# Emptying the transposed units of an attention backward: half by ScalarE and half by VectorE, or one whole unit by each

## The chip, the cores and the metric

The kernel runs on one core of a Trainium2 chip. The metric is the device time of one execution in microseconds (us). The engines are named as in the profile: PE is TensorE (PEld its weight loads), DVE is VectorE, ACT is ScalarE, POOL is GpSimd, SP is SyncE, which only issues transfers here. PSUM is the memory that TensorE writes to; SBUF is the working memory.

## The reference

The forward pass is a parallel transformer block on 2048 rows of 448 features, with 16 heads of 28; the kernel computes its output and the gradients of x and of five weight matrices.

```
xn  = layernorm(x)
q, k, v = split(xn @ wqkv)
p   = softmax(q k^T / sqrt(28));  o = p v
out = x + o @ wo + (silu(xn @ w_gate) * (xn @ w_up)) @ w_down
returns out and vjp(out)(grad_out) for x, wqkv, wo, w_gate, w_up, w_down
```

In the attention backward the scores and exp(scores) are computed again, and for each head ds = exp(scores) * (dO v^T - delta). From them come the sums for dv (exp with dO), dk (ds with q) and dq (ds with k). The last contracts over the keys, and for it ds is needed transposed.

## The kernel before

The program is one long list in which the order on each engine is written by hand; tile pools with a fixed number of buffers give the waits. It has three parts: the forward part with the feed-forward network (up to about 770 us of the profiled execution), the attention backward (about 770 to 1600 us), and a short end that makes dx. The change lies in the attention backward alone.

The backward works through 512 units in a loop over k (line 780). A unit is two heads, 512 keys and 128 query rows. Eight units make a group W; `pos` (0 to 7) is the place in the group; there are 64 groups. Unit k is spread over several turns of the loop:

- In turn k PE makes its scores into a PSUM tile `sd` (line 801, two matmuls on 32 rows each), and ScalarE makes E = exp (line 819).
- In turn k + 1 PE makes the product d of dO and v into another `sd` tile (line 814, two matmuls on the other 64 rows), and VectorE makes ds = d * E (line 831). There are three `sd` buffers.
- In turn k + 3 PE adds the unit to the sums for dv and dk (`acc_mm`, line 694, four matmuls in two pairs).

ds is transposed into `dsT` in two ways. Six units of a group go by a DMA transpose from SyncE's queue (line 833); `ds` has eight buffers, and a buffer is free again when its transpose has landed. The other two, units 1 and 4 (`TQ`), go by TensorE: `pe_transpose` makes eight 128x128 transposes into a PSUM tile `aux`, and `tr_out` copies it to SBUF. The early one (unit 1 of this group) comes at the end of position 6, and the late one (unit 4 of the group before) at position 0 between the scores and the d product.

The tile `aux` has a single buffer, and four uses take turns with it within a group: the late transposes at position 0; at positions 1 to 4 the fillers of a job (`job_mms`: a row block of the output `y`, a `dx` part with 14 matmuls of 448 columns, a part of the wqkv gradient `dwq`, or none), emptied by `job_out` on ScalarE; at position 5 the dq product (`dq_mm`), emptied by VectorE at position 6 (`dq_out`); then the early transposes. There are 16 groups with a `y` job, 32 with `dx`, 12 with `dwq`, and 4 without one.

SyncE's queue also carries the loads of the next chunks (`ck`, `x_c`, line 606 to 612), of the next pair and group (lines 582 and 590), and two more kinds of DMA transpose (lines 707 and 765). GpSimd's queue carries stores.

The functions that the change touches, and what calls them:

Of the kernel before, what the change touches and what calls it, by code (L numbers as in the profile page):

```python
# [37 lines left out]
def kernel(  # L38
# [19 lines left out]
    pe, act, dve, pool, sp = nc.tensor, nc.scalar, nc.vector, nc.gpsimd, nc.sync  # L58
# [70 lines left out]
    for c, (d0, dn) in enumerate(DCH):  # L129
        pool.tensor_copy(  # L130
            out=wq_sb[:dn, c].rearrange("p t g (hh r) -> p t (g hh) r", r=HP)[:, :, :, :DH],
            in_=wst[:dn, c, :].rearrange("p (t h d) -> p t h d", t=3, h=H))
# [4 lines left out]
    for hh in range(4):  # L137
        pool.dma_start(out=wo_pad[HP * hh:HP * hh + DH, :, :D], in_=wo_v[hh])
    dve.tensor_reduce(
        out=r_ones[:], in_=ident_f[:].rearrange("p (a b) -> p a b", b=HP)[:, :, 28:30],  # L140
# [102 lines left out]
    for b in range(4):  # L243
        sp.dma_start_transpose(
            out=dyT[:, 4 * b:4 * b + 4].rearrange("p t c s -> p (t c) s"),
            in_=dy_sp[:, 4 * b:4 * b + 4, :].rearrange("p t d -> p (t d)"))
# [238 lines left out]
    def load_w(nm, parts):  # L485

        t = wp.tile([P, NFC, D], BF16, name="W")
        src = {"wd": B_w_down.rearrange("(fc p) d -> p fc d", p=P), "wg": wT_d[0], "wu": wT_d[1], "wq": wqT_d}[nm]
        n = 3 * G if nm == "wq" else NFC
        wtile[nm] = t  # L490
        step = n // parts
        q = pool if nm == "wd" else sp
        out = [lambda i=i: q.dma_start(out=t[:, i:i + step, :], in_=src[:, i:i + step, :])
               for i in range(0, n, step)]
        return out
# [79 lines left out]
    def load_pair(pr, parts):  # L575

        g, r = pr // 2, 64 * (pr % 2)
        q = qdp.tile([P, S], BF16, name="QD")
        k = qdp.tile([P, S], BF16, name="KV")
        qd[pr] = (q, k)  # L580
        n = S // parts
        return [lambda i=i, dst=dst, r0=r0, src=src: sp.dma_start(
                    out=dst[r0:r0 + 64, i:i + n], in_=src[g, r:r + 64, i:i + n])
                for r0, srcs in ((0, (qT_d, kT_d)), (64, (dOT_d, vT_d)))
                for dst, src in zip((q, k), srcs) for i in range(0, S, n)]

    def load_group(g, parts):
        spt[g] = [spg.tile([P, NT, P], BF16, name=nm) for nm in ("Qsp", "Ksp", "dOsp")]
        n = NT // parts
        return [lambda i=i, t=t, src=src: sp.dma_start(  # L590
                    out=t[:, i:i + n, :].rearrange("p t c -> p (t c)"), in_=src[g, :, i * P:(i + n) * P])
                for t, src in zip(spt[g], (spq_d, spk_d, spo_d)) for i in range(0, NT, n)]
# [7 lines left out]
    def job_load(i):  # L600
        if i >= len(jobs) or jobs[i] is None:
            return
        j = jobs[i]
        if j[0] == "y":
            t = ckp.tile([P, NFC + G, P], BF16, name="ck")
            sp.dma_start(out=t[:], in_=hd_d[j[1], :, :G + NFC, :])
            x = ckp.tile([P, D], BF16, name="x_c")
            sp.dma_start(out=x[:], in_=x_d[:, j[1], :])
            chunk[i] = (t, x)
        elif j[0] == "dx":  # L610
            t = ckp.tile([P, NFC + G, P], BF16, name="ck")
            sp.dma_start(out=t[:, :NFC], in_=hd_d[j[2], :, G + NFC * (1 + j[1]):G + NFC * (2 + j[1]), :])
            chunk[i] = t
# [53 lines left out]
    def job_out(i, ps):  # L667
        j = jobs[i]
        if j[0] == "dwq":
            dwq_out(j[1], j[2], ps)  # L670
            return
        o = outp.tile([P, D], BF16, name="row_o")
        act.copy(out=o[:], in_=ps[:, :D])
        if j[0] == "y":
            pool.dma_start(out=out0_d[:, j[1], :], in_=o[:])
        else:
            pool.dma_start(out=(pA_d, pB_d)[j[1]][:, j[2], :], in_=o[:])
        if j[0] != "dwq" and j[-1] == NT - 1 and j[:2] != ("dx", 1):
            wload.extend(load_w("wg" if j[0] == "y" else "wu", 7))
# [34 lines left out]
    TQ = (1, 4)  # L714

    def pe_transpose(W, qi):

        ds, dsT = DS[W * UW + qi], st[("dsT", W)]
        ps = ps_x.tile([P, 8, P], BF16, name="aux")
        for i in range(8):  # L720
            pe.transpose(ps[:, i, :], ds[:, i // 4, (i % 4) * P:(i % 4 + 1) * P], ident_bf[:])  # L721
        st["tr"] = (ps, dsT[:, :, :, qi * P:(qi + 1) * P])

    def tr_out(eng):

        ps, dst = st["tr"]
        if eng is act:
            act.copy(out=dst[:, 0], in_=ps[:, 0:4, :])  # L728
        else:
            dve.tensor_copy(out=dst[:, 1], in_=ps[:, 4:8, :])  # L730

    def dq_mm(W, half):
        pr, kc, w, _ = units[W * UW]
# [46 lines left out]
    for k in range(N + 2 * UW):  # L780
        W, pos = k // UW, k % UW
        if k < N:
            pr, kc, w, qi = units[k]
            if k % 64 == 3 and pr + 1 < NPR:
                pload.extend(load_pair(pr + 1, 2))
            if k % 128 == 3 and pr + 2 < NPR:
                gload.extend(load_group(pr // 2 + 1, 2))
            if pos == 0:
                job_load(W + 2)
            if pos == 4:  # L790
                if W == len(jobs) - 1:
                    wload.extend(load_w("wq", 2))
                for lst, n in ((pload, 2), (gload, 1), (wload, 2)):
                    for f in lst[:n]:
                        f()
                    del lst[:n]
            q, kv = qd[pr]
            qt = 8 * w + qi
            s_ps = ps_sd.tile([P, 2, 512], FP32, name="sd")
            for j in range(2):  # L800
                pe.matmul(s_ps[:, j, :], lhsT=q[HP * j:HP * j + HP, qt * P:(qt + 1) * P],  # L801
                          rhs=kv[HP * j:HP * j + HP, kc * 512:(kc + 1) * 512],
                          start=True, stop=True, tile_position=(HP * j, 0))
        late_tr = pos == 0 and 1 <= W <= NW
        if late_tr:
            pe_transpose(W - 1, TQ[1])
        if 1 <= k <= N:
            pr, kc, w, qi = units[k - 1]
            q, kv = qd[pr]
            qt = 8 * w + qi  # L810
            d_ps = ps_sd.tile([P, 2, 512], FP32, name="sd")
            for j in range(2):
                r = 64 + HP * j
                pe.matmul(d_ps[:, j, :], lhsT=q[r:r + HP, qt * P:(qt + 1) * P],  # L814
                          rhs=kv[r:r + HP, kc * 512:(kc + 1) * 512],
                          start=True, stop=True, tile_position=(r, 0))
        if k < N:
            E[k] = ework.tile([P, 2, 512], BF16, name="E")
            act.activation(out=E[k][:], in_=s_ps[:], func=ACT.Exp, scale=SCALE)  # L819
        if late_tr:  # L820
            tr_out(act)
            tr_out(dve)
        job = jobs[W] if W < len(jobs) else None
        if pos == 6 and 2 <= W <= NW + 1:
            dq_out(W - 2)
        if 1 <= k <= N:
            if qi == 0:
                st[("dsT", (k - 1) // UW)] = twin.tile([P, 2, 4, UW * P], BF16, name="dsT")
            dsT = st[("dsT", (k - 1) // UW)]
            DS[k - 1] = dsw.tile([P, 2, 512], BF16, name="ds")  # L830
            dve.tensor_tensor(out=DS[k - 1][:], in0=d_ps[:], in1=E[k - 1][:], op=ALU.mult)  # L831
            if qi not in TQ:
                sp.dma_start_transpose(out=dsT[:, :, :, qi * P:(qi + 1) * P].rearrange("p j c q -> p (j c) q"),
                                       in_=DS[k - 1][:].rearrange("p j c -> p (j c)"))
        while sp_later:
            sp_later.pop(0)()

        if pos == 1:
            if 3 <= k < N + 3:
                acc_mm(k - 3)  # L840
            if job:
                st["aux"] = ps_x.tile([P, 512], FP32, name="aux")
                fillers = job_mms(W, st["aux"])
        if 1 <= pos < 5 and job:
            n = -(-len(fillers) // (5 - pos))
            for f in fillers[:n]:
                f()
            fillers = fillers[n:]
        if pos == 5 and 2 <= W <= NW + 1:
            dq_mm(W - 2, 0)  # L850
            dq_mm(W - 2, 1)
        if pos != 1 and 3 <= k < N + 3:
            acc_mm(k - 3)
        if pos == 4 and job:
            job_out(W, st["aux"])
        if pos == 6 and W < NW:
            pe_transpose(W, TQ[0])
            tr_out(act)
            tr_out(dve)
    while sp_later:  # L860
        sp_later.pop(0)()
# [3 lines left out]
    with ExitStack() as fin:  # L865
# [17 lines left out]
        for c in range(4):  # L883
            ps = ps_sd.tile([P, 2, 512], FP32, name="sd")
# [68 lines left out]
```

## Time and profile before

| what | value |
|---|---|
| time, median of 3 runs | 1677.39 us (1677.09 to 1687.07) |
| profiled execution: its time, its span | 1683.64 us, 1681.9 us |
| mean granted TensorE clock | 0.952 |
| busy share of the span: PE, PEld, DVE, ACT, POOL | 90%, 36%, 67%, 71%, 24% |
| ScalarE halves of the copies (L728) | 128 of 595 ns, 76.2 us |
| VectorE halves of the copies (L730) | 128 of 424 ns, 54.3 us |
| DMA transposes of ds on SyncE's queue (L833) | 384, median 4.1 us from issue to landing |

Lines of the profile name a group of instructions by the line of the kernel, the engine, the operation and the tiles (out<-in), then the count, the busy time, the mean length in ns, and the time that the engine was idle just before them with what ended it. A line of the timeline has the start and the length in us; x2 after it means that two instructions in a row were put together.

### The profile page before, as it was taken

How to read it: one execution, taken by the hardware profiler on the slowest of the kernel's cores; microseconds unless marked ns; L12 is line 12 of the kernel's file. 1: busy time of each engine (PE TensorE's matmuls, PEld its weight loads, DVE VectorE, ACT ScalarE, POOL GpSimd, SP SyncE). 2: the span in 40 equal slices, each digit the busy share in tenths (PEclk: the TensorE clock that was granted, in tenths of full speed). 3: DMA queues.
4: the chain of work that ended last, by engine and by line, in shares of the span. 5: the costliest groups of instructions: out<-in, count | busy, mean ns of one | idle time of the engine just before them, and what ended most of it. 6: DMA issues, size and time to landing. Idle time of an engine off the chain costs nothing. (4 is left out here: it accounts for less than half of the span.)

```text
span 1681.9 us, 32121 instructions
## 1 busy us (share of the span) xinstructions
PE 1519.8 (90%) x12176; PEld 600.7 (36%) x12176; DVE 1131.8 (67%) x1530; ACT 1186.3 (71%) x1346; POOL 400.9 (24%) x664
## 2 busy tenths in 40 slices
PE   3699999999999999696998999999989999999875
PEld 1132333333233333232443335443335433544352
DVE  6365555555555456345887788888878888888736
ACT  2497888888777678574776777777777777777611
POOL 4133334344234333421001101010102101111132
PEclk9699999999998899797999989999999999999998
DMA  4785658687866577548999999999999999999963
GB/s 126 145 181 115 133 121 169 140 169 118 157 131 130 124 136 148 138 93 231 214 208 212 196 175 196 207 196 208 206 202 194 202 202 179 175 195 195 175 239 100
DMA packets 682155, 285.13 MB, mean 170 GB/s; under 512 B 637792, under 2 KB 651088, under 8 KB 682000
## 3 DMA queue, kind: packets, MB, share of 16 engines
q1 hardware_dynamic: 653616, 215.74, 68.7%
q0 software_dynamic: 25808, 64.30, 15.4%
q10 hardware_dynamic: 2576, 3.04, 0.6%
q8 instruction: 95, 1.56, 0.4%
q14 instruction: 60, 0.49, 0.1%
HBM read 67.34 MB, written 63.44 MB: 78 GB/s over the span
## 5 line engine op out<-in xcount | busy, mean ns | idle before, releaser
L831 DVE TENSOR_TENSOR ds<-sd,E 128x1024 bf16<-128x1024 f32 x512 | 607.6, 1217 | 81.5 <-PE sd L814 34.2
L819 ACT ACTIVATE E<-sd 128x1024 bf16<-128x1024 f32 x512 | 520.1, 1031 | 193.4 <-PE sd L814 99.0
L535 ACT ACTIVATE eT<-s_ps 128x1024 bf16<-128x1024 f32 x512 | 518.2, 1025 | 159.8 <-PE s_ps L531 154.5
L801 PE MATMUL sd<-KV,QD 32*128 32x512 bf16 x1024 | 202.1, 391 | 19.2 <-DVE ds L831 8.1
L814 PE MATMUL sd<-KV,QD 32*128 32x512 bf16 x1024 | 202.9, 388 | 10.9 <-DVE ds L831 6.8
L694 PE MATMUL acc<-ds,Qsp 128*32 128x512 bf16 x1024 | 204.5, 395 | 1.2 <-DVE ds L831 1.2
L531 PE MATMUL s_ps<-qT,kT 32*128 32x512 bf16 x1024 | 204.7, 397 | 0.0
L694 PE MATMUL acc<-E,dOsp 128*32 128x512 bf16 x1024 | 204.3, 395 | 0.0
L339 PE MATMUL f_ps<-xnT,wgu 128*128 128x512 bf16 x448 | 135.9, 400 | 24.7 <-DVE w_sb L365 13.0
L378 POOL DMA_DIRECT2D hd_d<-fT x168 | 126.9, 769 | 40.9 <-DVE fT L363 24.9
L531 PEld LDWEIGHTS <-kT 32*128 32x128 bf16 x1024 | 48.2, 91 | 203.7 <-issue 201.7
L664 PE MATMUL aux<-W,ck 128*128 128x448 bf16 x448 | 106.6, 354 | 6.9 <-DVE dsT L730 6.9
L313 PE MATMUL f_ps<-xn_sp,f_sp 128*128 128x448 bf16 x448 | 110.6, 355 | 0.0
L709 POOL DMA_DIRECT2D dqkv_d<-dkv_o x64 | 39.2, 617 | 284.9 <-ACT dkv_o L700 284.8
L801 PEld LDWEIGHTS <-QD 32*128 32x128 bf16 x1024 | 50.2, 91 | 149.0 <-issue 140.5
L511 PE MATMUL o_ps<-eT,v_sp 128*32 128x512 bf16 x1024 | 101.7, 399 | 0.0
L730 DVE COPY dsT<-aux 128x512 bf16<-128x512 bf16 x128 | 54.3, 424 | 61.7 <-ACT dsT L728 61.7
L694 PEld LDWEIGHTS <-dOsp 128*32 128x32 bf16 x1024 | 50.3, 94 | 120.3 <-issue 117.3
L814 PEld LDWEIGHTS <-QD 32*128 32x128 bf16 x1024 | 69.4, 91 | 53.4 <-issue 34.2
L721 PE MATMUL aux<-ident_bf,ds 128*128 128x128 bf16 x1024 | 78.5, 219 | 11.0 <-DVE dq_acc L758 3.5
L743 PE MATMUL aux<-dsT,Ksp 128*32 128x512 bf16 x1024 | 78.3, 405 | 4.1 <-DMA dsT<-ds 2.5
L351 DVE SCALAR_TENSOR_TENSOR g<-t_sb,f_ps 128x512 f32<-128x512 f32 x56 | 38.4, 686 | 64.6 <-ACT t_sb L349 64.5
(130 smaller groups left out, 1803.1 us busy)
## 6 DMA issues: line engine op xcount, KB each, us to landing
hd_d<-fT POOLq DMA_DIRECT2D x168, 128.0 KB, 4.0
ck<-hd_d SPq DMA_DIRECT2D x32, 448.0 KB, 4.2
ck<-hd_d SPq DMA_DIRECT2D x16, 576.0 KB, 5.0
dsT<-ds SPq DMA_TRANSPOSE x384, 4.1
dq_c<-dqkv_d SPq DMA_DIRECT2D x8, 768.0 KB, 4.7
dqkv_d<-dkv_o POOLq DMA_DIRECT2D x64, 64.0 KB, 3.5
W<-wT_d SPq DMA_DIRECT2D x14, 224.0 KB, 3.9
out_dram<-dw_o POOLq DMA_DIRECT2D x28, 96.0 KB, 4.1
```

Source lines behind the costliest of these rows:

```text
L313: pe.matmul(acc[:, :D], lhsT=src[:, 12 * (t // 4) + 4 * wi + t % 4, :], rhs=rhs[:, t, :D], start=(t == 0), stop=(t == NT - 1))
L339: pe.matmul(st[name][:], lhsT=w(c), rhs=src[:, tsl, c, :], start=(c == 0), stop=(c == 3))
L378: pool.dma_start(out=hd_d[tsl, :, G + NFC * wi + fc, :].rearrange("k p s -> p k s"), in_=o[:, wi, :].rearrange("p (k s) -> p k s", k=4))
L511: pe.matmul(o_ps[HP * hh:HP * (hh + 1), :], lhsT=v[:, kt, HP * hh:HP * (hh + 1)], rhs=e[hh // 2][:, hh % 2, :], start=(kt == 0), stop=(kt ...
L531: pe.matmul(s_ps[:, j, :], lhsT=kT[r:r + HP, kt * P:(kt + 1) * P], rhs=qT[r:r + HP, qc * 512:(qc + 1) * 512], start=True, stop=True, tile_ ...
L535: act.activation(out=e[:], in_=s_ps[:], func=ACT.Exp, scale=SCALE)
L664: return [lambda n=n: pe.matmul(ps[:, :D], lhsT=t[:, n, :], rhs=w[:, n, :], start=(n == 0), stop=(n == NFC - 1)) for n in range(NFC)]
L694: pe.matmul(acc[r:r + HP, :], lhsT=src[:, qt, 64 * hp + HP * j:64 * hp + HP * j + HP], rhs=m[:, j, :], start=(qt == 0), stop=(qt == NT - 1 ...
L801: pe.matmul(s_ps[:, j, :], lhsT=q[HP * j:HP * j + HP, qt * P:(qt + 1) * P], rhs=kv[HP * j:HP * j + HP, kc * 512:(kc + 1) * 512], start=Tru ...
L814: pe.matmul(d_ps[:, j, :], lhsT=q[r:r + HP, qt * P:(qt + 1) * P], rhs=kv[r:r + HP, kc * 512:(kc + 1) * 512], start=True, stop=True, tile_p ...
L819: act.activation(out=E[k][:], in_=s_ps[:], func=ACT.Exp, scale=SCALE)
L831: dve.tensor_tensor(out=DS[k - 1][:], in0=d_ps[:], in1=E[k - 1][:], op=ALU.mult)
```

## The change

`tr_out` now copies all eight transposed blocks with one instruction, on the engine that it is given. The early unit's copy is left to VectorE alone and the late unit's to ScalarE alone. At position 0 the late transposes are issued on PE after the d product of the unit before, not between the scores and that product, so that the two score products (scores and d) stand side by side on PE.

```diff
     def tr_out(eng):
 
         ps, dst = st["tr"]
-        if eng is act:
-            act.copy(out=dst[:, 0], in_=ps[:, 0:4, :])
-        else:
-            dve.tensor_copy(out=dst[:, 1], in_=ps[:, 4:8, :])
+        out, in_ = dst.rearrange("p j c q -> p (j c) q"), ps[:]
+        act.copy(out=out, in_=in_) if eng is act else dve.tensor_copy(out=out, in_=in_)
...
         late_tr = pos == 0 and 1 <= W <= NW
-        if late_tr:
-            pe_transpose(W - 1, TQ[1])
         if 1 <= k <= N:
...
                 pe.matmul(d_ps[:, j, :], lhsT=q[r:r + HP, qt * P:(qt + 1) * P],
                           rhs=kv[r:r + HP, kc * 512:(kc + 1) * 512],
                           start=True, stop=True, tile_position=(r, 0))
+        if late_tr:
+            pe_transpose(W - 1, TQ[1])
         if k < N:
             E[k] = ework.tile([P, 2, 512], BF16, name="E")
             act.activation(out=E[k][:], in_=s_ps[:], func=ACT.Exp, scale=SCALE)
         if late_tr:
             tr_out(act)
-            tr_out(dve)
...
         if pos == 6 and W < NW:
             pe_transpose(W, TQ[0])
-            tr_out(act)
             tr_out(dve)
```

## The prediction

> **What bounds the kernel now.** The change touches only the attention backward, from 780 us to 1590 us of the span, so I first read busy time by stage (columns: stretch, its length, then busy us of PE, PEld, DVE, ACT and POOL, granted clock, DMA share, GB/s). Two of its stretches of eight groups:
>
> ```profile
> 1293.00:1395.00 102.00, 94.97 (x978) 43.12 (x974) 85.85 (x89) 77.36 (x92) 14.15 (x32) 1.00 1.10 202
> 1493.00:1590.00 97.00, 92.28 (x859) 38.16 (x859) 85.79 (x89) 75.07 (x89) 11.27 (x19) 0.98 1.05 193
> ```
>
> PE is 93 to 95% busy, but modelled ends hide waits; nothing else is full, except perhaps the DMA engines. The groups of the backward give the two halves of the copies, and VectorE's waits what the second half waits for:
>
> ```profile
> L728 ACT COPY dsT<-aux 128x512 bf16<-128x512 bf16 x128 | 76.2, 595 | 8.1 <-PE aux L721 7.4 <-DMA x_c<-in_A_x_dram 0.5
> L730 DVE COPY dsT<-aux 128x512 bf16<-128x512 bf16 x128 | 54.3, 424 | 61.7 <-ACT dsT L728 61.7
> DVE dsT L730 <- ACT dsT L728: 61.7, 128, 0.8
> DVE ds L831 <- PE sd L814: 26.8, 64, 2.6
> DVE ds L831 <- DMA dsT<-ds: 23.5, 22, 2.2
> ```
>
> VectorE's half never runs beside ScalarE's: all 128 wait for it. Next, the timeline where one group passes into the next (start, length):
>
> ```profile
> 1488.72 0.39 PE L801 MATMUL sd<-KV,QD 32*128 32x512 bf16 x2
> 1488.83 0.58 ACT L728 COPY dsT<-aux 128x512 bf16<-128x512 bf16 x1
> 1488.99 0.39 PE L814 MATMUL sd<-KV,QD 32*128 32x512 bf16 x2
> 1489.31 1.95 ACT L819 ACTIVATE E<-sd 128x1024 bf16<-128x1024 f32 x2
> 1489.44 0.42 DVE L730 COPY dsT<-aux 128x512 bf16<-128x512 bf16 x1 [0.19 <-ACT dsT L728]
> 1489.64 0.39 PE L801 MATMUL sd<-KV,QD 32*128 32x512 bf16 x2
> 1489.96 0.62 PE L721 MATMUL aux<-ident_bf,ds 128*128 128x128 bf16 x8
> 1490.52 0.39 PE L814 MATMUL sd<-KV,QD 32*128 32x512 bf16 x2
> 1491.12 0.61 ACT L728 COPY dsT<-aux 128x512 bf16<-128x512 bf16 x1
> 1491.77 0.42 DVE L730 COPY dsT<-aux 128x512 bf16<-128x512 bf16 x1 [0.77 <-ACT dsT L728]
> 1492.24 0.92 PE L664 MATMUL aux<-W,ck 128*128 128x448 bf16 x4 [0.21 <-DVE dsT L730]
> ```
>
> From the first score product of position 7 (1488.72) to the first filler at position 1 (1492.24), which waits for the `aux` buffer, are 3.52 us. The path is: early copy, two exps (1489.31 to 1491.26), late ScalarE copy, late VectorE copy (to 1492.19), filler. I measured this stretch at several other boundaries, crowded ones too, and found 3.52 to 3.57. This chain, not PE's work, sets the pace there. Last, SyncE's queue in a crowded stretch, and VectorE beside it:
>
> ```profile
> 1324.14 5.45 SPq L833 DMA_TRANSPOSE dsT<-ds  x3
> 1329.68 1.22 SPq L707 DMA_TRANSPOSE dkv_sp<-dkv_o  x1
> 1330.96 1.22 SPq L582 DMA_DIRECT2D QD<-dOT_d  x2
> 1332.28 4.05 SPq L833 DMA_TRANSPOSE dsT<-ds  x3
> 1336.42 0.54 SPq L612 DMA_DIRECT2D ck<-hd_d  x1
> 1336.07 2.36 DVE L831 TENSOR_TENSOR ds<-sd,E 128x1024 bf16<-128x1024 f32 x2 [1.88 <-DMA dsT<-ds]
> ```
>
> SyncE issues almost without a hole: these pieces and the small gaps between them fill 1324.14 to 1336.96. VectorE waits 1.88 us for a `ds` buffer whose DMA transpose is late. So there is a second pace-maker, and a group saved in such a stretch is waited for again.
>
> **The change, part by part.** Per group it removes two ScalarE halves and two VectorE halves, and adds one whole copy on each. It moves eight transposes behind the d product. It moves no DMA and nothing on SyncE's or GpSimd's queue.
>
> *Whole VectorE copy (early unit).* Not in the trace. The f32 rows L758 (512 columns, 681 ns) and L831 (1024, 1217 ns) give 536 ns for 512 more columns and a fixed 145 ns. The bf16 half took 424, so 279 of it is for columns, and the whole is 145 + 2 x 279 = 0.70 us. Bounds: 0.42 (second half free) and 0.96 (second half at the f32 rate). It replaces a wait and a half. The transposes start at 1488.18 and can be read 0.64 later, at 1488.82; VectorE is in ds until 1489.25; copy 1489.18 (neighbours overlap by 0.08) to 1489.88; next ds 1489.80, against 1489.79 now. Worth nothing; at 0.96 that ds is 0.26 late, covered because the following ds then has over a microsecond to spare.
>
> *Whole ScalarE copy (late unit).* Exp of 1024 columns takes 1.03, and L637 to L673 (384 to 448 columns, 476 to 528 ns) show 0.81 ns a column, which from 595 makes 1.01. I take 1.04. Bounds: 0.87 (595 + VectorE's 279) and 1.19 (two halves, fixed part twice).
>
> *The chain after.* Without the early copy on ScalarE, exp of position 7 starts 0.43 after its scores (the lag in the trace where ScalarE is free): 1489.15, not 1489.31, ending 1490.18. The d product waits for that exp (its PSUM buffer) and starts 0.05 later, at 1490.23, not 1490.52. The transposes are now behind it: 1490.23 + 0.32 = 1490.55, not 1489.96. Queued behind the waiting d on PE stand these transposes, one acc block and the next score products; the last have 0.2 us to spare. Transposes readable +0.64 = 1491.19 (ScalarE's next exp has ended by 1491.11), copy +1.04 = 1492.23, filler +0.05 = 1492.28. Now: 1492.24. So the chain gets 0.04 us *longer*.
>
> *Adjacent scores.* Apart, s and d take PE 0.32 each; adjacent (as elsewhere) 0.33 together. That is 0.32 us of PE a group, hidden behind the chain: PE waits for `aux` anyway. Without that cover, 63 x 0.32 = 20 us.
>
> *What is gained.* At position 2 s starts at 1493.10 but d at 1493.38, behind the ds that ended 1493.32, late because of the late VectorE copy. That copy goes, and this ds starts 1.2 us earlier. What is late next is exp of position 1, now behind the whole copy: 1492.13 to 1493.17, so d at 1493.22. Gain 0.16 us in each of 32 dx groups. In the 12 dwq groups the fillers are 0.13 longer, so d goes about at once: gain 0.20. In the 16 y groups s and d are 0.09 apart already: about 0. Groups without a job: 0. Sum: 32 x 0.16 + 12 x 0.20 = 7.5 us. I count in full only the 13 dx and 4 dwq groups after the last crowded stretch (2.1 + 0.8 = 2.9); of the other 4.6 I count half, since their transposes then queue longer at SyncE. Together 5 us, which makes 1683.6 into 1678.6 for the profiled execution. That one lies 6.3 above the median, so by the median 1677.4 - 5 = 1672.4 us.
>
> [...] If the halves did run side by side, the late evacuation before would be 0.61 us and the whole copy would cost 0.43 x 60, some 26 us; by the row a pair takes 0.61 + 0.03 + 0.42 = 1.06 and the whole about the same.
>
> **Rivals.** (a) *PE decides.* For it: 93 to 95% busy. Then the 20 us of separate scores come out: 1657. Against: the constant 3.52, with the filler waiting on `aux`. (b) *SyncE's queue takes all.* For: 22 waits for DMA transposes, 23.5 us. Every gain is returned: 1677. Against: the last 17 groups have almost none of these waits. (c) *The whole ScalarE copy is dear.* Each 0.1 us above 1.04 lengthens the chain in 60 groups by 6 us; beyond 1.04 + 7.5/60 = 1.17 all gain is gone. At 1.19, dx and dwq lie about even and the y groups lose 0.19 x 16 = 3 us: 1680. To be slower by 1% (17 us) it needs about 1.45 us, or the late transposes held up as much by d. For: ScalarE already paces that chain. Against: every 1024-column exp takes 1.03. (d) *The change is as good as absent:* its early half is, by the timeline above (1489.80 against 1489.79), so everything rests on the late unit; 1677, with (b).
>
> **How the numbers follow.** Forecast (a gain of 2 to 10 us) 0.50; (b) and (d) together 0.18; (a) 0.12; (c) with a loss under 1% 0.12, over 1% 0.08. The range goes from 1662 (copy at 0.87, which is 10 us, and half the rest) to 1686: (c) at 1.19 plus some 6 us, the distance of the profiled execution from the median. One per cent, 17 us, is about what a measurement of this kernel can tell from no change; faster by more 0.12, within 0.78, slower by more 0.10.
>
> **What would show it.** Right: 64 whole copies near 1.04 us on ScalarE and 0.70 on VectorE; 61.7 us of waits for ScalarE's copy gone; the stretch from position 7's scores to the first filler at 3.5 to 3.6; d at position 2 about 0.1 after s in dx groups; VectorE's waits for DMA transposes at or above 23.5 us. Wrong: that stretch under 3.3 or over 3.8, groups without DMA waits shorter than 11.8 us, or a ScalarE copy above 1.2.

## The result, and the profile after

The changed kernel takes 1676.05 us (median of 20 runs, 1668.56 to 1680.84). The kernel before, run beside it, takes 1682.2 us (median of 20, 1676.83 to 1691.75). The ratio is 0.996 with a 95% interval of 0.9944 to 0.9976, so the gain is some 6.7 us by the ratio: 0.4%, well inside the 1% that counts as no change here, though the interval leaves out 1. The forecast was 1672.4 us by a gain of 5.

The profiled execution of after has 1668.56 us and a span of 1666.8, which is 15.1 us less than the profiled execution of before. That is not the gain. About 5 us of it lie ahead of the backward, which the change does not touch: the first ds starts at 763.8 us, and at 768.9 before. Over the fourteen profiles of this study that start lies anywhere from 760.2 to 769.1. So I read what a single stretch costs from the traces, and what a kernel costs from the medians.

The groups of the backward have the new copies, one line for each engine:

```profile
L728 ACT COPY dsT<-aux 128x1024 bf16<-128x1024 bf16 x64 | 64.8, 1012 | 8.9 <-PE aux L721 1.6 <-DMA dsT<-ds 0.5
L728 DVE COPY dsT<-aux 128x1024 bf16<-128x1024 bf16 x64 | 43.5, 679 | 0.0
```

64 copies on each, of 1012 and 679 ns. The last column is the idle time before them: VectorE's copy waits for nobody any more, where its half stood idle for 61.7 us behind ScalarE's. VectorE's waits in the same stretch of time:

```profile
DVE ds L828 <- PE sd L810: 58.9, 117, 5.3
DVE ds L828 <- DMA dsT<-ds: 42.0, 34, 3.6
```

The 61.7 us did not become speed. The wait for d products went from 26.8 to 58.9 us, since VectorE is now simply early, and the wait for DMA transposes went from 23.5 to 42.0 us. Whether the second line costs something is what the experiments below try.

The timeline at one passage from group to group (start, length; three dots stand for lines in between):

```profile
1498.29 0.39 PE L799 MATMUL sd<-KV,QD 32*128 32x512 bf16 x2
...
1498.72 1.95 ACT L817 ACTIVATE E<-sd 128x1024 bf16<-128x1024 f32 x2 [0.21 <-PE sd L799]
1498.74 0.68 DVE L728 COPY dsT<-aux 128x1024 bf16<-128x1024 bf16 x1
...
1499.79 0.39 PE L810 MATMUL sd<-KV,QD 32*128 32x512 bf16 x2 [0.19 <-ACT E L817]
...
1500.11 0.62 PE L721 MATMUL aux<-ident_bf,ds 128*128 128x128 bf16 x8
...
1500.77 1.01 ACT L728 COPY dsT<-aux 128x1024 bf16<-128x1024 bf16 x1
...
1501.83 0.92 PE L664 MATMUL aux<-W,ck 128*128 128x448 bf16 x4
...
1502.68 0.39 PE L799 MATMUL sd<-KV,QD 32*128 32x512 bf16 x2
1502.76 0.39 PE L810 MATMUL sd<-KV,QD 32*128 32x512 bf16 x2
```

Counted from position 7's scores at 1498.29: exp at +0.43, d at +1.50, transposes at +1.82, copy at +2.48, first filler at +3.54. The prediction had +0.43, +1.51, +1.83, +2.47 and +3.56. At position 2 (the last two lines) d follows s by 0.08 us, where it was 0.28.

### The profile page after: what moved, and what is told of

Read it like the earlier page. It is cut to its first block, busy times and chain, and to the rows that moved or that the text cites. A ratio compares the mean times of both kernels' runs of the same rounds, so it can differ in the third digit from the quotient of the medians.

```text
span 1666.8 us, 31996 instructions
## 1 busy us (share of the span) xinstructions
PE 1489.6 (89%) x12176; PEld 588.6 (35%) x12176; DVE 1122.9 (67%) x1466; ACT 1191.6 (71%) x1282; POOL 400.8 (24%) x664
## 2 busy tenths in 40 slices
DMA packets 682153, 285.11 MB, mean 171 GB/s; under 512 B 637792, under 2 KB 651088, under 8 KB 682000
## 3 DMA queue, kind: packets, MB, share of 16 engines
q0 software_dynamic: 25808, 64.30, 15.2%
## 4 chain that ended last, share of the span: by engine, by line
PE 64%; DMA 13%; DVE 7%; ACT 7%; issue 5%; SPq 1%; POOL 1%; DVEq 0%; POOLq 0%; ACTq 0%
PE s_ps L531 9%; PE f_ps L339 9%; DMA dsT<-ds 9%; PE f_ps L313 9%; PE sd L799 5%; PE o_ps L511 5%; PE aux L664 4%; ACT E L817 4%; PE acc L694 4%; PE aux L741 3%; DVE ds L828 3%; PE aux L721 3%; PE aux L658 3%; PE f_ps L157 3%; ACT dsT L728 3%
## 5 line engine op out<-in xcount | busy, mean ns | idle before, releaser
L799 PEld LDWEIGHTS <-QD 32*128 32x128 bf16 x1024 | 50.6, 91 | 147.7 <-issue 139.0
L694 PEld LDWEIGHTS <-dOsp 128*32 128x32 bf16 x1024 | 50.2, 93 | 112.1 <-issue 102.1
L810 PEld LDWEIGHTS <-QD 32*128 32x128 bf16 x1024 | 65.2, 91 | 64.5 <-issue 60.2
L741 PE MATMUL aux<-dsT,Ksp 128*32 128x512 bf16 x1024 | 74.2, 387 | 6.1 <-DMA dsT<-ds 4.6
L313 PEld LDWEIGHTS <-f_sp 128*128 128x128 bf16 x672 | 51.2, 98 | 76.0 <-issue 45.8
```

Source lines behind the costliest of these rows:

```text
L313: pe.matmul(acc[:, :D], lhsT=src[:, 12 * (t // 4) + 4 * wi + t % 4, :], rhs=rhs[:, t, :D], start=(t == 0), stop=(t == NT - 1))
L694: pe.matmul(acc[r:r + HP, :], lhsT=src[:, qt, 64 * hp + HP * j:64 * hp + HP * j + HP], rhs=m[:, j, :], start=(qt == 0), stop=(qt == NT - 1 ...
```

## The experiments

The runs were taken in three sets (e1 to e4, e5 to e8, e9 to e12), each on one chip with runs of the kernel before beside them. In the table, "chain" is the stretch of the prediction (position 7's scores to the first filler, median over the passages into a group with a job), "d - s" the lag at position 2 in dx groups, and "DMA waits" VectorE's waits for DMA transposes of ds in the backward. Ratios are to the kernel before in the same set.

| kernel | median us | ratio, 95% interval | chain us | d - s us | DMA waits us |
|---|---|---|---|---|---|
| before | 1682.2 | 1 | 3.52 | 0.28 | 23.5 |
| after | 1676.05 | 0.996 (0.9944 to 0.9976) | 3.55 | 0.08 | 42.0 |
| e1_copies | 1672.6 | 0.9947 (0.9925 to 0.9968) | 3.32 | 0.08 | 50.2 |
| e2_move | 1686.18 | 1.0023 (1.0005 to 1.0041) | 3.74 | 0.28 | 18.7 |
| e3_swap | 1690.66 | 1.0058 (1.0036 to 1.0079) | 3.96 | 0.13 | 16.4 |
| e4_extra | 1689.51 | 1.0046 (1.0025 to 1.0068) | 4.17 | 0.01 | 11.0 |
| e5_before_pool | 1706.83 | 1.0158 (1.0120 to 1.0196) | 3.52 | 0.28 | 38.0 |
| e6_after_pool | 1706.41 | 1.0162 (1.0131 to 1.0192) | 3.55 | 0.08 | 77.8 |
| e7_copies_pool | 1705.52 | 1.0145 (1.0108 to 1.0181) | 3.33 | 0.08 | 90.9 |
| e8_copies_ds12 | 1674.55 | 0.9969 (0.9949 to 0.9990) | 3.33 | 0.08 | 23.8 |
| e9_before_noload | 1656.32 | 0.9868 (0.9848 to 0.9889) | 3.52 | 0.28 | 0.3 |
| e10_after_noload | 1646.65 | 0.9811 (0.9796 to 0.9827) | 3.55 | 0.08 | 3.9 |
| e11_copies_noload | 1635.43 | 0.9748 (0.9732 to 0.9763) | 3.33 | 0.08 | 4.6 |
| e12_extra_noload | 1679.65 | 1.0006 (0.9990 to 1.0022) | 4.17 | 0.01 | 1.5 |

### First: the two halves of the change apart, and the copy's price

The theory is that of the prediction: the chain sets the pace at each passage, and what a kernel gains follows from its length. The rival is that PE's own work does, so that adjacent score products are what pays.

**e1_copies** has the whole copies alone. The late transposes stay where they were before the change, between s and d:

```diff
 # against after
         late_tr = pos == 0 and 1 <= W <= NW
+        if late_tr:
+            pe_transpose(W - 1, TQ[1])
         if 1 <= k <= N:
...
-        if late_tr:
-            pe_transpose(W - 1, TQ[1])
```

> Whole copies as in the change, but the late transposes stay between the scores and the d product as before. Theory (the chain from position 7's scores to the first filler sets the pace): the transposes start 0.32 us after position 0's scores, without waiting for position 7's exp, are readable before ScalarE is free, and the whole copy follows the second exp at once; the chain is 3.33 us instead of 3.55 after the change and 3.52 before. That is 0.2 us in each of 60 groups, 12 us, of which SyncE's queue takes about half: some 6 us faster than the changed kernel, ratio to before about 0.993. Rival (PE sets the pace, the adjacent scores were the gain): the 0.32 us of the separate pairs come back, some 20 us slower than the changed kernel, ratio to before about 1.008.

Its timeline at a passage:

```profile
1481.60 0.39 PE L799 MATMUL sd<-KV,QD 32*128 32x512 bf16 x2
...
1482.84 0.62 PE L721 MATMUL aux<-ident_bf,ds 128*128 128x128 bf16 x8
...
1483.87 1.01 ACT L728 COPY dsT<-aux 128x1024 bf16<-128x1024 bf16 x1
...
1484.93 0.35 PE L664 MATMUL aux<-W,ck 128*128 128x448 bf16 x1 [0.16 <-ACT dsT L728]
```

The transposes are done early (+1.24 instead of +1.82), the copy starts when exp of the new unit has ended, and the filler comes at +3.33 and names the copy as what it waited for. The chain is 0.22 us shorter than after's, as the theory says. The adjacency that it gives up costs nothing that can be seen: it isn't slower than after. Whether it is faster stays open, since 0.9947 and 0.996 have overlapping intervals. With DMA waits of 50.2 us it shows where the missing part may be.

**e2_move** is the other half: halves as before, with the late transposes behind d.

```diff
 # against before
-        if late_tr:
-            pe_transpose(W - 1, TQ[1])
         if 1 <= k <= N:
...
+        if late_tr:
+            pe_transpose(W - 1, TQ[1])
         if k < N:
```

> The halves as before, but the late transposes moved behind the d product. Theory (chain): position 7's exp stands behind the early ScalarE half, d waits for it, the transposes for d, and then both halves follow one after the other: the chain is about 3.75 us, and the ds that position 2 waits for starts behind the late VectorE half. About 0.25 us a group, 15 us slower than before, ratio about 1.008. Rival (PE sets the pace): adjacent scores save 0.32 us a group, ratio about 0.988.

The chain came at 3.74 and the kernel is slower, 0.2% with an interval that leaves out 1. Here the scores are adjacent and nothing is won by it: the rival with PE falls. VectorE's wait for ScalarE's half has grown with the chain, from 61.7 to 77.6 us:

```profile
DVE dsT L730 <- ACT dsT L728: 77.6, 125, 1.7
DVE ds L831 <- PE sd L812: 35.5, 72, 6.3
DVE ds L831 <- DMA dsT<-ds: 18.7, 18, 2.0
```

**e3_swap** exchanges the engines: the early unit's copy on ScalarE, the late one's on VectorE.

```diff
 # against after
         if late_tr:
-            tr_out(act)
+            tr_out(dve)
...
             pe_transpose(W, TQ[0])
-            tr_out(dve)
+            tr_out(act)
```

> The change with the engines exchanged: the early unit whole on ScalarE, the late unit whole on VectorE. Theory (chain): the early copy of 1.01 us stands ahead of position 7's exp, which starts at 1.03 instead of 0.43 us after its scores, and everything behind it moves; the late VectorE copy stands ahead of a ds. Chain about 3.8 us, some 0.3 us a group slower than before, ratio about 1.01. Rival (only that the second half's wait is gone matters, not which engine takes which unit): as the change, 0.996.

The copy itself is about 0.3 us shorter on VectorE, and the kernel is slower than before by 0.6%: the chain came at 3.96. Its timeline at a passage shows where it grew:

```profile
1520.42 0.39 PE L799 MATMUL sd<-KV,QD 32*128 32x512 bf16 x2
...
1520.53 1.01 ACT L728 COPY dsT<-aux 128x1024 bf16<-128x1024 bf16 x1
...
1521.43 1.95 ACT L817 ACTIVATE E<-sd 128x1024 bf16<-128x1024 f32 x2
...
1522.84 0.62 PE L721 MATMUL aux<-ident_bf,ds 128*128 128x128 bf16 x8
...
1523.50 0.69 DVE L728 COPY dsT<-aux 128x1024 bf16<-128x1024 bf16 x1 [1.10 <-PE aux L721]
...
1524.38 0.93 PE L664 MATMUL aux<-W,ck 128*128 128x448 bf16 x4
```

The early copy, now on ScalarE, stands ahead of position 7's exp. That exp starts at +1.01 instead of +0.43, and the late transposes behind it start at +2.42 instead of +1.82. The shorter late copy gives back 0.3 us, and the filler follows it after 0.19 instead of 0.05. VectorE stands idle before the late copy until the transposes are there:

```profile
DVE dsT L728 <- PE aux L721: 76.3, 63, 1.9
```

That is 76.3 us of waiting in 63 copies. The choice of engine matters by what has to wait behind the copy, not by the copy's speed.

**e4_extra** is after with a suspected cost added: ScalarE copies the late unit's first half once more, into the same place.

```diff
 # against after
         if late_tr:
             tr_out(act)
+            ps_, dst_ = st["tr"]
+            act.copy(out=dst_[:, 0], in_=ps_[:, 0:4, :])
```

> The change, and ScalarE copies the first half of the late unit a second time (0.6 us of work that changes nothing). Theory (chain): the chain gets 0.5 us longer in 60 groups, up to 30 us; in the crowded quarter of the groups some of it is hidden behind SyncE: 22 to 30 us slower than the changed kernel, ratio to before 1.009 to 1.014. Rival (PE sets the pace): hidden, as the change, 0.996. Rival (SyncE's queue sets the pace): under 10 us.

Its groups show the extra copy (first line; the last column is 2.0 us of idle time) and the fillers of the dx groups, whose idle time of 23.4 us is put down to it for 21.9:

```profile
L821 ACT COPY dsT<-aux 128x512 bf16<-128x512 bf16 x63 | 36.9, 585 | 2.0
L664 PE MATMUL aux<-W,ck 128*128 128x448 bf16 x448 | 107.7, 357 | 23.4 <-ACT dsT L821 21.9 <-DMA KV<-kT_d 0.7 <-DMA dsT<-ds 0.7
```

36.9 us of ScalarE's time lengthen the chain by 0.62 us (3.55 to 4.17), and the kernel by about 0.9%, 14 us against after: 1.0046 against 0.996. ScalarE is on the path, but only some 14 of the 37 us arrive at the end.

So in this set the chains came close to what was worked out, and e1 to e4 all lie on the side of before that their chains say. The sizes are smaller. Sixty times the chain's difference to before would make e1 12 us faster and e2, e3 and e4 13, 26 and 39 us slower; by the ratios they are 9 faster and 4, 10 and 8 slower. (The change itself, whose chain is 0.03 us longer than before, is faster all the same; where that comes from is read below, at position 2 and in the groups without a job.) The DMA waits run the other way: 11.0 us where the chain is 4.17, 50.2 where it is 3.32. What a short chain wins is in part waited for at the transposes.

### Second: is it SyncE's issue queue?

The prediction named SyncE's queue, which issues almost without a hole, as the second pace-maker. If its issue time is the limit, then moving the loads of the jobs to GpSimd's queue frees it. **e5_before_pool**, **e6_after_pool** and **e7_copies_pool** do that to before, after and e1_copies:

```diff
 # the same three edits against before, after and e1_copies
-            sp.dma_start(out=t[:], in_=hd_d[j[1], :, :G + NFC, :])
+            pool.dma_start(out=t[:], in_=hd_d[j[1], :, :G + NFC, :])
...
-            sp.dma_start(out=x[:], in_=x_d[:, j[1], :])
+            pool.dma_start(out=x[:], in_=x_d[:, j[1], :])
...
-            sp.dma_start(out=t[:, :NFC], in_=hd_d[j[2], :, G + NFC * (1 + j[1]):G + NFC * (2 + j[1]), :])
+            pool.dma_start(out=t[:, :NFC], in_=hd_d[j[2], :, G + NFC * (1 + j[1]):G + NFC * (2 + j[1]), :])
```

> The kernel before, but the loads of the job chunks (48 of ck, 16 of x_c) are issued from GpSimd's queue, not SyncE's: some 40 us less issue time on SyncE. Groups at the length of the quiet ones would make the backward some 27 us shorter than it was. If SyncE's issue time is the second limit: 8 to 27 us faster, ratio 0.984 to 0.995. If the DMA engines themselves are (the transposes then stretch as before, whoever issues the loads): about 1.0.

> The changed kernel with the job loads on GpSimd's queue. If SyncE's issue time took part of the change's gain, the change is worth more here: the chain and position 2 promise 7.5 us (and the jobless groups some more) against the kernel before with the same loads, not the 6 measured; 10 to 30 us faster than the changed kernel, ratio to before 0.979 to 0.990. If the DMA engines limit: 0.996.

> Whole copies, the late transposes between scores and d, and the job loads on GpSimd's queue. With SyncE relieved the 0.23 us a group that the shorter chain saves against the change should come out nearly whole: 8 to 14 us faster than the changed kernel with the same loads, ratio to before 0.972 to 0.984. If the DMA engines limit: as whole copies alone, 0.995.

All three became slower, by about 1.5%, and level: 1706.83, 1706.41 and 1705.52 us. The chain at the passages is unchanged in each, yet its length no longer shows: by the chain e7 would be 13 us ahead of e6, and it is 0.9. First after, then e6_after_pool: the transposes of ds on SyncE's queue (length in ns: least, median, greatest) and the time from issue to landing.

```profile
L830 SPq DMA_TRANSPOSE dsT<-ds x381: 1231/1294/4852, 780.0 to 1574.6; - x191
...
DMA to landing us min/median/max: 3.1/4.1/8.7
```

```profile
L830 SPq DMA_TRANSPOSE dsT<-ds x358: 1231/1296/8840, 779.4 to 1578.8; - x179
...
DMA to landing us min/median/max: 3.0/4.3/13.9
```

The median is the same and the tail is not: one issue took up to 8.8 us, one landing up to 13.9. The mean of an issue was 1.49 us before the change, 1.53 after it, and 1.65, 1.70 and 1.71 in these three. SyncE has less to issue and the slow transposes take longer. So what this tail adds isn't SyncE's own issue work; it looks as if a transpose is held up by something further down, which a load from another queue disturbs more, not less. These three runs don't show what that is, since the move changed more than the queue: the same 26 MB went in 5632 packets instead of 9216, and a 448 KB load of `ck` took 5.7 us to land in e6 where it took 4.4 in after. TensorE also ran longer at half its clock in the backward, 44, 65 and 61 us in these three profiles against 31, 24 and 24 in before, after and e1_copies. Whether that is a part of the cause or follows from the waits was not tried.

**e8_copies_ds12** tries the buffers: e1_copies with twelve `ds` buffers instead of eight, so that VectorE can run further ahead of late transposes.

```diff
 # against e1_copies
-    dsw = ast.enter_context(tc.tile_pool(name="dsw", bufs=8))
+    dsw = ast.enter_context(tc.tile_pool(name="dsw", bufs=12))
```

> Whole copies, the late transposes between scores and d, with 12 buffers of ds instead of 8. The 50.6 us of waits for DMA transposes fall below 25. But SyncE had only some 8 us of idle time left in this kernel's backward: if its throughput is the limit, the time falls by no more than 8 us, ratio to before 0.990 to 0.995, and the wait shows up elsewhere (at the dq product, for dsT). If only the bursts were the trouble: 20 us or more, under 0.983.

The time is that of e1_copies (0.9969 and 0.9947, intervals overlapping). VectorE's waits for transposes are halved, from 50.2 to 23.8 us, but PE's waits for the same transposes, ahead of the dq products, grow from 2.7 us in e1_copies to this:

```profile
PE aux L741 <- DMA dsT<-ds: 9.3, 4, 5.4
```

PE's other waits for transfers (`dq_sp` and the weights `W`) grow too, from 6.1 to 16.0 us. So of the 26 us that VectorE waits less, some 16 turn up as waits on PE, and the time stays. More buffers mostly move the wait.

### Third: the bytes taken out

If the transposes are held up at the DMA engines, which they share with the loads (in after, from 790 to 1580 us, the shares of the 16 engines' time are 99.9% for the packets of SyncE's queue and 6.8% for those of GpSimd's), then taking away the bytes must free them whatever queue issued them. **e9_before_noload**, **e10_after_noload**, **e11_copies_noload** and **e12_extra_noload** are before, after, e1_copies and e4_extra in which only the first job's chunk is loaded and every job uses that one; the y and dx parts are therefore not those of the reference. The page's DMA total falls from 285.11 MB in after to 259.85 MB, by 25 MB. The issue time of these loads on SyncE, some 37 us, goes with them. All instructions of the compute engines stay.

```diff
 # the same edit against before, after, e1_copies and e4_extra
         if j[0] == "y":
-            t = ckp.tile([P, NFC + G, P], BF16, name="ck")
-            sp.dma_start(out=t[:], in_=hd_d[j[1], :, :G + NFC, :])
-            x = ckp.tile([P, D], BF16, name="x_c")
-            sp.dma_start(out=x[:], in_=x_d[:, j[1], :])
-            chunk[i] = (t, x)
+            if i == 0:
+                t = ckp.tile([P, NFC + G, P], BF16, name="ck")
...
+                one_load.append((t, x))
+            chunk[i] = one_load[0]
         elif j[0] == "dx":
-            t = ckp.tile([P, NFC + G, P], BF16, name="ck")
...
+            chunk[i] = one_load[0][0]
```

> The kernel before, but only the first job's chunk is loaded and every job multiplies that one, so 47 loads of ck and 15 of x_c are left out (y and the dx parts are not those of the reference). That takes about 22 MB out of the DMA engines and nothing out of the other engines. If the DMA engines with the transposes on them are the second limit, every group runs as the quiet ones do: some 25 us faster, ratio about 0.985, and VectorE's waits for DMA transposes near 0. If they aren't, 1.0.

> The changed kernel with the job loads left out in the same way. If the DMA engines took part of the gain, it comes out here: groups at the length of the quiet ones of the changed kernel (dx 11.9, dwq 12.0, y 12.5, jobless 10.7) make the backward 757 us, 44 shorter than before; ratio about 0.974, 17 us ahead of the kernel before with the loads left out. If the change is worth only what was measured, 6 us ahead.

> Whole copies with the late transposes between scores and d, job loads left out. The chain is 0.22 us shorter than after the change and now nothing takes that away: 60 x 0.2 = 12 us ahead of the changed kernel with the loads left out, ratio about 0.967. If PE or the DMA engines still limit: level with it.

> The changed kernel with ScalarE's first half copied once more, job loads left out. The chain was 4.17 us with this copy, 0.62 above the change. With the DMA engines relieved each group pays it whole: 60 x 0.6 = 36 us slower than the changed kernel with the loads left out, ratio about 0.995. If the copy is partly hidden by something other than the DMA engines, as with the loads: some 15 us slower, 0.983.

VectorE's waits in e10_after_noload, where after had 42.0 us:

```profile
DVE ds L830 <- PE sd L812: 63.3, 144, 6.4
...
DVE ds L830 <- DMA dsT<-ds: 3.9, 6, 1.0
```

The waits for transposes are all but gone in all four, and for e11 and e12 the sizes are now those of the chain. The change is worth 9.7 us (1656.32 to 1646.65), where it was 6.7 with the loads. e11, with a chain 0.22 us shorter, is another 11.2 us ahead (60 x 0.22 is 13), where with the loads e1 could not be told from after. And the extra ScalarE copy of e12 costs 33.0 us (1646.65 to 1679.65), nearly the 37 us that 60 x 0.62 makes, where with the loads 14 arrived. The groups say the same one by one: from e10 to e11 a group gets 0.19 to 0.25 us shorter in the median, by the kind of its job, and from e10 to e12 0.54 to 0.62 longer. The waits in e12_extra_noload say whom VectorE follows there:

```profile
DVE ds L832 <- ACT E L819: 63.1, 60, 1.3
```

So the chain through ScalarE sets the pace of the groups with a job when transposes arrive in time, and the loads beside the transposes cap what a shorter chain may bring. Both sets relieve SyncE of the issue of these loads, e5 to e7 by moving them and e9 to e12 by leaving them out, and only the second helps. That speaks for the DMA engines and against the issue queue, and so does the time from issue to landing of a transpose, 4.1 us in the median before and 3.6 in e9. It isn't a full proof: loads from GpSimd's queue may do harm of their own that hides what the relief of SyncE brings, and bytes, the number of transfers and SyncE's issue time all went together in e9 to e12.

## Why the prediction was right, and where it was not

**The chain.** Right, piece by piece. It forecast 3.56 us at the passage and after has 3.55 as the median; no instant of it was off by more than 0.02. It rested on the finding that the second half never ran beside the first, and e1 and e2 show the two parts of it apart: whole copies alone make 3.32, the move alone 3.74. Against 3.52 these are -0.20 and +0.22 us, which add up, but for rounding, to the +0.03 of after: the move takes back what the copies win at the passage. What kept the halves apart is in the trace too: each of the 128 VectorE halves waits for a semaphore that ScalarE's half sets (and starts 0.03 us after that half's end), so the order is one of the program, and no run here shows the halves without it.

**The whole copies.** 1.04 and 0.70 us were taken; 1.012 and 0.679 were measured, both inside the bounds. Scaling the column part of the half copy and leaving the fixed part alone was enough. Had the halves run side by side, the other case that the prediction weighed, the whole ScalarE copy would have lengthened each passage by 0.43 us by its estimate; with the copies alone, in e1, the passage is 0.20 us shorter.

**Adjacent scores at nothing.** Right. e2 has them and is slower, e1 hasn't and is not. The 20 us of rival (a) were never there.

**The gain at position 2.** The mechanism is right: d follows s by 0.08 us in dx groups, by 0.28 before. It comes with the whole copies, as said: e1 has 0.08, and e2, with the halves, 0.28. In groups without DMA waits the period fell from 12.16 and 12.07 us, which alternate, to 11.98 and 11.85, so 0.18 to 0.22 us instead of 0.16. The dwq groups, compared one by one, gained 0.11 in the median with loads and 0.16 without, where 0.20 was put. y groups gained 0.08 without loads (12.59 to 12.51), where about 0 was put. All small.

**Groups without a job: the step that failed.** They were put at 0. Three of them (the fourth is the last group of all) went from 13.2, 13.4 and 13.1 us to 10.9, 11.1 and 10.9, about 2.2 us each and together as much as the whole measured gain. At 10.9 us they also lie under the 11.8 us that the prediction named as a sign of being wrong. The group behind the first two gives back some 3 us of it (15.2 to 18.3): its dwq fillers wait for a transposed dq, which this group reaches sooner. PE's wait for it, first before, then after:

```profile
PE aux L627 <- DMA dq_sp<-dq_o: 1.6, 1, 1.6
```

```profile
PE aux L627 <- DMA dq_sp<-dq_o: 4.3, 1, 4.3
```

So these three groups together took 41.9 us before and 40.4 after. The windows view shows what differs. Its columns are the stretch, its length, the busy us (and count) of PE, PEld, DVE, ACT and POOL, the granted clock, the DMA share and GB/s; first before, then after:

```profile
985.00:1011.00 26.00, 23.49 (x192) 8.22 (x191) 20.93 (x22) 17.86 (x22) 3.62 (x6) 0.74 1.02 183
1420.00:1433.00 13.00, 12.58 (x114) 4.88 (x112) 10.65 (x12) 8.98 (x11) 1.20 (x2) 0.74 0.86 164
```

```profile
980.00:1002.00 22.00, 18.54 (x196) 7.29 (x193) 20.90 (x21) 18.46 (x21) 3.62 (x6) 1.00 1.06 192
1407.00:1418.00 11.00, 9.06 (x97) 3.52 (x97) 10.48 (x11) 9.33 (x11) 1.20 (x2) 1.00 1.10 170
```

A mean clock of 0.74 means that TensorE ran at half speed for about half of each such group (a share h at 0.5 gives 1 - h/2 = 0.74, so h is 0.52: 6.8 of 13 us). After ran them at 1.00. The length of such a group goes with this. In the changed order it takes 10.9 us at full speed, 11.7 with 3.41 us at half (the third group of e10) and 12.9 with 6.83 us (the third of e6); in the order of before it takes 12.3 with 3.41 us (the first of e9) and 12.8 to 13.5 with 6.83. So most of the 2.2 us is the clock. Why it holds in one order and falls in the other was not tried and stays open. With the loads on SyncE's queue, e1 keeps full speed there too, and the kernels with a longer chain than before, e2 to e4, have 3.4 to 6.8 us at half speed in each of these groups. But the changed order doesn't always keep it up: the groups of e6 and e10 just named fell, and after itself has 6.83 us at half speed in the group with the wait of 4.3 us.

In the traces of before and after the granted clock is 0.5 or 1 throughout. From 790 us to the last ds, before has six half-speed stretches of 3.41 or 6.83 us, 30.7 us together; after has five of the same two lengths, 23.9 us together.

**What the second pace-maker takes back.** That something takes back is right; the place is most likely wrong, and the size isn't settled. The prediction took 4.6 us of the gain at half, 2.3 of 7.5, because transposes would queue longer at SyncE. Measured, the gain is 9.7 us without loads and 6.7 with them. That would be 3 of 9.7 taken back, but the intervals of the two gains (about 4 us either way without loads, about 3 with them) overlap. Clear of noise is what the loads take in the other kernels: the extra copy costs 33 us without them and 14 with them. It is hardly SyncE's issuing, which e5 to e7 relieved and made things worse; e9 to e12 freed the transposes by taking the loads out. Rival (b) is thus the right kind of limit, most likely in the wrong place, and it doesn't take all.

**The sum.** 5 us were forecast and 6.7 measured. That they agree is partly luck: the jobless groups bring about 6.7 - 3 = 3.7 us that were not in the sum, and single stretches add up to more than the medians give. The parts that were in the sum came out near it: between the profiles of before and after the dx groups are 4.3 us shorter together, where 5.1 was put, and the dwq groups other than the one that waits 3.1, where 2.4 was put. Between the profiles of e9 and e10 the stretch from the first ds to the last shortened by 15.6 us (798.4 to 782.8), and the part behind it lengthened by 4.8 (91.1 to 95.9), which together is near the 9.7 of the medians. With the loads the two are 12.5 us shorter and 2.5 longer. Whether that tail is given back for a reason, or is scatter (it lies between 88.2 and 99.1 us over all profiles), stays open.

**Rival (c).** The copy's price was not reached, but the way it would have gone is shown. e4 adds 0.62 us to the chain and is slower than before by 0.5%, and e12 shows that without the DMA waits the same copy costs 33 us.

## What to carry to other kernels

Work out the chain from one engine to the next with its starts, not the engines' busy sums: here a copy of 1.01 us on one engine replaced two halves of 0.60 and 0.42 that never ran together, because one waited for the other's semaphore, and a wait of 61.7 us went away for a gain of 6.7. Then ask what shared transfer comes due sooner when that chain gets shorter, and test that limit by taking out its bytes as well as by changing the queue that issues them, since the two gave opposite signs. And read the granted clock of groups with little work on PE apart from the others: here their mean was 0.74 in one order and mostly 1.00 in the other, and that made up about half of the measured gain.

## What the runs showed of the hardware that was not expected

Moving 64 loads (48 of `ck`, 16 of `x_c`) from SyncE's to GpSimd's queue, with the same bytes, cost 1.5% (some 26 us) and stretched single DMA transposes of a 128x1024 tile to 8.8 us at issue, where the median is 1.3 and the longest was 4.9 in after. The transposes' mean issue length differed with the loads beside them: 1.40 us with the loads taken out of before, 1.49 with them on SyncE, 1.65 with them on GpSimd.

Half-speed stretches of TensorE appeared in a steady loop whose PE was still 90% busy by the page's count (23.49 of 26.00 us), in the groups without fillers; the busy count includes the slower matmuls themselves (in after a matmul of the sums for dv and dk lasts 0.39 us at full speed and 0.61 in a half-speed stretch), so it hides the loss.
